# Windowed attention and a bilinear feed-forward layer: four more down projections by seven block products, with up weights and sums of w_out parked in HBM

## The chip, the cores and the metric

The kernel runs on one core of a Trainium2 chip. The metric is the device time of one execution in microseconds (us); the median of three runs of the kernel before is 953.4 us (953.39 to 955.16). Batches, blocks and products are counted from 0 in this text: the change concerns the down projections of batches 3, 4, 5 and 6 of 8, which are the fourth to the seventh.

## The reference

Eight batches with 8 heads, 576 tokens and 64 columns a head go through attention with a window of 128 tokens, and the result, 4608 tokens of 512 numbers, through a bilinear layer with 1536 hidden columns. All in float32.

```python
scores = scale * np.matmul(q, k.transpose(0, 1, 3, 2))
...
scores = np.where(mask, scores + bias[None], -1000000000.0)
...
return np.matmul(attn, v).astype(np.float32)
...
a = x @ w_a
b = x @ w_b
return (a * b @ w_out).astype(np.float32)
```

## The kernel before

**Numbers.** A float32 operand is split into two float16 numbers, a high and a low one, and each product of two such operands is three float16 matmuls. The token dimension of a batch is cut into two halves of `HT` = 288 tokens, so nearly every matmul of the layer is 128x128 weights by 288 columns.

**Stages of a batch.** Attention works on pairs of heads, four pairs a batch, and runs ahead of the layer. The *up* stage forms for each of 12 hidden blocks `f` both products with `w_a` and `w_b` and multiplies them (`up_fast`, line 1187). From batch 2 on it does this by seven block products of half size in place of eight (Strassen's scheme in Winograd's form): `wup[:, f]` holds seven operands for block f, the four given ones and three sums, each as high and low. `up` runs two lanes, the even and the odd blocks, interleaved. The *down* stage multiplies the hidden numbers with `w_out` (`wdn`). For batches 0 to 6 it does so directly (`down`, line 1257): 2 token halves x 4 output blocks x 12 hidden blocks x 3 = 288 matmuls. The last batch alone uses seven products there too (`down_fast`, line 1357): 7 x 2 x 6 x 3 = 252 matmuls. For this `Pairs.keep` (line 1324) forms, for each pair of hidden blocks, sums of their halves, called tops, and writes them over up weights that the last batch does not need again; `Pairs.weights` (line 1293) forms sums of w_out in buffers that attention no longer needs.

**After each product** ScalarE (ACT) or VectorE (DVE) takes the result out of PSUM. In the plain path `halve` (line 1145) then splits a hidden block with one ACT cast and one DVE subtraction of 2x288.

**What sets the order.** Every operation is recorded first (`Plan.record`), so all instructions carry one line of the program, 353; tiles tell them apart. `Plan.order` lists them by priorities (due times worked back from the end) and estimated costs, `arrange` (line 336) tries three settings of `early` with some repetitions each and keeps the best, and `emit` writes the instructions out in order of planned start. On the chip each engine runs its own list in that order and waits by semaphores. SyncE (SP) issues nearly all DMAs: an entry that waits holds back all entries behind it. `weave` and `att.along` set how attention, up and down are recorded beside each other.

**Names in rows.** `ch` and `ef` are PSUM banks of up and down, `at` those of attention; `rc`, `row` hold hidden numbers in float32, `stage` (also called h) the split hidden numbers of a batch, `xs` the split attention output, `phl` the split probabilities, `pT` their transposes by DMA, `qk`, `qkh`, `qkl`, `qst`, `v`, `vhl` the inputs of attention and their halves.

## Time and profile before

| | |
|---|---|
| runs | 955.16, 953.40, 953.39 us |
| the profiled execution | 953.69 us, of which its span is 951.9 us |
| TensorE (PE) busy | 938.8 us, 99% of the span, 9317 matmuls in the record |
| VectorE (DVE) busy | 721.6 us, 76% |
| ScalarE (ACT) busy | 652.4 us, 69% |
| GpSimd (POOL) busy | 277.7 us, 29% |
| mean granted TensorE clock | 0.996 of full speed |
| HBM read, written | 48.33 MB, 9.44 MB |

The profiled execution took 1.8 us more than its span and lies 0.3 us above the median. A busy time is the union of an engine's instructions; on DVE the recorded instructions overlap a little, so a group's mean is longer than the distance from one start to the next. Some matmul records can be missing.

### The profile page before, as it was taken

How to read it: one execution, taken by the hardware profiler on the slowest of the kernel's cores; microseconds unless marked ns; L12 is line 12 of the kernel's file. 1: busy time of each engine (PE TensorE's matmuls, PEld its weight loads, DVE VectorE, ACT ScalarE, POOL GpSimd, SP SyncE). 2: the span in 40 equal slices, each digit the busy share in tenths (PEclk: the TensorE clock that was granted, in tenths of full speed). 3: DMA queues.
4: the chain of work that ended last, by engine and by line, in shares of the span. 5: the costliest groups of instructions: out<-in, count | busy, mean ns of one | idle time of the engine just before them, and what ended most of it. 6: DMA issues, size and time to landing. Idle time of an engine off the chain costs nothing.

```text
span 951.9 us, 23890 instructions
## 1 busy us (share of the span) xinstructions
PE 938.8 (99%) x9317; PEld 742.3 (78%) x9317; DVE 721.6 (76%) x1955; ACT 652.4 (69%) x1737; POOL 277.7 (29%) x336
## 2 busy tenths in 40 slices
PE   7999999999999999999999999999999999999998
PEld 5777777777877877777777778778777777877776
DVE  4999998985888889956877577857767567488860
ACT  5979987676777777777757766777657766434431
POOL 1201021061677576301223122301222022362210
PEclk8999999999999999999999999999999999999999
DMA  9638563449536423554438344274336352200001
GB/s 355 189 126 275 157 133 106 155 86 217 131 78 183 96 46 80 111 155 101 89 56 213 71 98 95 71 180 94 72 71 134 117 93 32 49 33 7 2 7 45
DMA packets 150737, 104.90 MB, mean 110 GB/s; under 512 B 120160, under 2 KB 130016, under 8 KB 149728
## 3 DMA queue, kind: packets, MB, share of 16 engines
q1 hardware_dynamic: 141120, 93.83, 40.6%
q10 hardware_dynamic: 9504, 9.54, 3.1%
q8 instruction: 73, 1.20, 0.5%
q14 instruction: 40, 0.33, 0.1%
HBM read 48.33 MB, written 9.44 MB: 61 GB/s over the span
## 4 chain that ended last, share of the span: by engine, by line
PE 92%; DVE 3%; DMA 2%; issue 1%; ACT 1%; SPq 0%; DVEq 0%; ACTq 0%
PE ch L353 42%; PE ef L353 40%; PE at L353 11%; DMA qk<-in_kT 1%; DVE wup L353 1%; DMA stage<-in_kT 1%; DMA wdn<-in_w_b 1%; DVE small L353 0%; SPq L353 0%; DVE t L353 0%; DVE rc L353 0%; ACT qkh L353 0%; DVE qkl L353 0%; DVE xs L353 0%; ACT sq L353 0%
## 5 line engine op out<-in xcount | busy, mean ns | idle before, releaser
L353 PEld LDWEIGHTS <-wup 128*128 128x128 f16 x4176 | 403.1, 98 | 111.3 <-issue 4.5
L353 PE MATMUL ch<-xs,wup 128*128 128x288 f16 x2184 | 307.7, 286 | 0.7 <-ACT row L353 0.6
L353 PE MATMUL ef<-xs,wup 128*128 128x288 f16 x1992 | 284.7, 286 | 1.9 <-DVE wup L353 1.9
L353 PEld LDWEIGHTS <-wdn 128*128 128x128 f16 x2124 | 204.5, 98 | 54.6
L353 PE MATMUL ef<-stage,wdn 128*128 128x288 f16 x1080 | 138.1, 286 | 0.0
L353 ACT ACTIVATE t<-t,small 128x192 f32<-128x192 f32 (+2 forms) x276 | 118.3, 431 | 22.3 <-DVE small L353 21.7
L353 PE MATMUL ch<-stage,wdn 128*128 128x288 f16 x1008 | 130.1, 286 | 0.0
L353 DVE SCALAR_TENSOR_TENSOR phl<-t,small,phl 128x192 f16<-128x192 f32 (+2 forms) x252 | 109.0, 474 | 10.3 <-ACT phl L353 9.5
L353 POOL TENSOR_TENSOR rc<-rc,row 128x288 f32<-128x288 f32 x60 | 55.4, 923 | 209.9 <-DVE row L353 170.7
L353 ACT ACTIVATE phl<-t,small 128x192 f16<-128x192 f32 (+2 forms) x252 | 91.9, 427 | 6.6 <-DVE small L353 4.7
L353 DVE CUSTOM_DVE_ANT_0 t<-at,bias,small 128x192 f32<-128x192 f32 (+2 forms) x216 | 74.0, 390 | 21.1 <-PE at L353 20.3
L353 POOL TENSOR_TENSOR wup<-wup 128x128 f32<-128x128 f32 (+1 forms) x110 | 80.8, 760 | 25.6 <-DVE wup L353 17.0
L353 ACT ACTIVATE row<-ch,small 128x288 f32<-128x288 f32 x99 | 49.0, 495 | 54.9 <-PE ch L353 52.1
L353 ACT CAST stage<-rc 128x576 f16<-128x576 f32 (+1 forms) x81 | 52.3, 646 | 40.2 <-DVE rc L353 31.9
L353 DVE TENSOR_TENSOR stage<-rc,stage 128x576 f16<-128x576 f32 (+1 forms) x81 | 63.4, 782 | 7.5 <-ACT stage L353 6.3
L353 DVE SCALAR_TENSOR_TENSOR rc<-rc,small,ch 128x288 f32<-128x288 f32 x79 | 40.2, 509 | 32.7 <-PE ch L353 31.2
L353 POOL TENSOR_SCALAR bias<-rel_sb,small,sl_sb 128x192 f32<-128x192 f32 x24 | 19.3, 805 | 128.5 <-DVE small L353 128.5
L353 POOL TENSOR_TENSOR v<-v 128x576 f32<-128x576 f32 x24 | 34.9, 1453 | 60.6 <-ACT v L353 38.0
L353 ACT ACTIVATION_READ_ACCUMULATOR t<-t,small 128x1 f32 x276 | 52.5, 190 | 0.0
L353 DVE TENSOR_TENSOR xs<-v,xs 128x576 f16<-128x576 f32 x48 | 45.8, 973 | 8.3 <-ACT xs L353 8.3
L353 DVE SCALAR_TENSOR_TENSOR qkl<-qk,small,qkh 128x1152 f16<-128x1152 f32 x24 | 35.8, 1491 | 15.0 <-ACT qkh L353 13.1
L353 PEld LDWEIGHTS <-vhl 128*64 128x64 f16 x1176 | 39.9, 110 | 6.7 <-issue 6.4
(168 smaller groups left out, 1250.1 us busy)
## 6 DMA issues: line engine op xcount, KB each, us to landing
v<-in_vP SPq DMA_DIRECT2D x7, 1280.0 KB, 7.2
out<-row ACTq DMA_DIRECT2D x56, 144.0 KB, 2.7
qk<-in_qT SPq DMA_DIRECT2D x24, 288.0 KB, 4.0
qk<-in_kT SPq DMA_DIRECT2D x24, 288.0 KB, 4.7
wdn<-in_w_a SPq DMA_DIRECT2D x12, 512.0 KB, 6.3
wdn<-in_w_b SPq DMA_DIRECT2D x12, 512.0 KB, 8.0
wdn<-in_w_out SPq DMA_DIRECT2D x12, 512.0 KB, 6.0
qst<-qkh SPq DMA_DIRECT2D x24, 144.0 KB, 3.0
```

The lines of the kernel that those rows point to most:

```text
L353: getattr(eng, fn)(*args, **kw)
```

## The change

1. **Down by seven products from batch 3 on** (`Pairs.FIRST = 3`, `batch`). `up_fast` of these batches writes into `pair` tiles and calls `pairs.keep` in place of `halve`; `down_fast` gets all seven products in a new order, and its results leave through `stage` space, by SP's queue for all but the last batch.
2. **Up weights go to HBM and come back.** The tops of batches 3 to 7 are written over up blocks 1, 3, 5 and 7, the sums of w_out over blocks 6, 8 and 9. So these blocks (7 DMAs, 41 pieces of 131,072 bytes, 5.37 MB) are saved once while their sums are formed (`save`), and brought back after the down stages of batches 2 to 6 (`restore`, five times).
3. **Sums of w_out** are formed once, in batch 2's down stage, by DVE and ACT in up blocks already read, stored to HBM, and fetched again for each down stage (`fetch`, 3 DMAs, 2.36 MB, five times); one sixth of them stays in `wdn` from batch 3 on (`fetch_lasts`, 6 DMAs).
4. **The planner**: prices for DMAs that also count eight completion lanes, the bytes of each transfer and some stalls; a load from the parked copies may start up to 20 us ahead of its due time, others 100 us; and after the old trials 60 more with changed due times, of which the best stays.
5. **Rest**: `xs`, `rc` and the new `pair` tiles share one tile `rows`; the second half of the plain down outputs goes by SP from `stage` space; temporary places of the up sums are listed by hand (`turns`); the token scale's sums use an attention bank in paired batches.

```diff
 class Plan:
-            u.cost, u.lat = (4900.0, 4100.0) if kw.get("transpose") else (450.0, 4000.0)
+            u.ahead = 20000.0 if any(x.tensor.name in self.scratch for x in ins) else 100000.0
+            u.cost, u.lat = (4900.0, 4100.0) if kw.get("transpose") else (450.0, 3500.0 + u.line)
...
+        for n in range(60):
+            order, dues, self.zero, self.early = best[1]
+            dues = dict(dues)
+            for v, x in best[3]:
+                if rng.random() < 0.2:
+                    dues[v] -= x * rng.random() * 2
+            self.order(order, dues)
+            if self.end < best[0]:
+                best = keep()
...
     class Pairs:
+        FIRST = 3
+        TOPS, WEIGHTS = ((1, 0), (3, 0), (3, 1), (5, 0), (5, 1), (7, 0)), (6, 8, 9)
+        KEPT = ((1, 5), (3, 7), (5, 7), (7, 4), (6, 6), (8, 6), (9, 6))
+        UNIT = 512
...
+        def restore(self):
+            for f, k, to in self.blocks:
+                sp.dma_start(self.part(f, k), to)
+
+        def fetch(self, b):
+            for f, x in zip(self.WEIGHTS, self.loads):
+                sp.dma_start(self.part(f, 6), x)
...
         def weights(self):
...
+                for k, x in enumerate((a, c)):
+                    vec.tensor_tensor(out=x, in0=wdn[:, 2 * i + k, 0, :], in1=wdn[:, 2 * i + k, 1, :], op=ALU.add)
+                a11, a21, a12, a22 = (x[:, e:e + 256] for x in (a, c) for e in (0, 256))
+                vec.tensor_tensor(out=a22, in0=a21, in1=a22, op=ALU.add)
+                vec.tensor_tensor(out=a21, in0=a11, in1=a21, op=ALU.subtract)
+                vec.tensor_tensor(out=a11, in0=a22, in1=a11, op=ALU.subtract)
+                vec.tensor_tensor(out=a12, in0=a12, in1=a11, op=ALU.subtract)
                 yield
+                for z, w in ((a12, to[4]), (a22, to[2]), (a21, to[3]), (a11, to[1])):
+                    act.copy(w[:, 0, :], z)
+                    vec.tensor_tensor(out=w[:, 1, :], in0=z, in1=w[:, 0, :], op=ALU.subtract)
+                sp.dma_start(self.loads[i // 2][:, 3 * n * (i % 2):3 * n * (i % 2) + 3 * n], flat[:, n:4 * n])
+                sp.dma_start(self.lasts[:, i * n:i * n + n], flat[:, 4 * n:5 * n])
...
         def keep(self, f):
...
-            act.copy(tops[:, :, 0, :], x)
-            for n in (0, 2):
-                vec.tensor_tensor(out=tops[:, n:n + 2, 1, :], in0=x[:, n:n + 2, :], in1=tops[:, n:n + 2, 0, :], op=ALU.subtract)
+            first, rest = self.top(i, 0), self.top(i, slice(1, 4))
+            act.copy(first[:, 0, :], x[:, 0, :])
+            vec.tensor_tensor(out=first[:, 1, :], in0=x[:, 0, :], in1=first[:, 0, :], op=ALU.subtract)
+            act.copy(rest[:, :, 0, :], x[:, 1:4, :])
+            vec.tensor_tensor(out=rest[:, :, 1, :], in0=x[:, 1:4, :], in1=rest[:, :, 0, :], op=ALU.subtract)
...
     def down_fast(b, oi, p):
+        p.fetch(b)
...
+        yield from p.product(pss[0], 4, 0, True, True)
...
+        for j in range(2):
+            yield from p.product(chs[j], 5, j, False, True)
+            act.activation(xx[j][2], chs[j], AF.Copy, scale=oi)
...
+        yield from p.product(pss[1], 4, 1, True, True)
...
+        for j in range(2):
+            yield from p.product(pss[j], 2, j, False, True)
...
+        for j in range(2):
+            yield from p.product(chs[j], 3, j, False, True)
...
+        for j in range(2):
+            yield from p.product(chs[j], 6, j, False, True)
+            act.activation(xx[j][3], chs[j], AF.Copy, scale=oi)
+            out(j, 1, xx[j][3])
+        if b < B - 1:
+            p.restore()
...
     def batch(b):
+        paired = b >= pairs.FIRST
+        if b == pairs.FIRST:
+            pairs.fetch_lasts()
+        ups = up(states[b], None if paired else h, plain, fast)
...
+        if paired:
+            weave(att.along(down_fast(b, out_scale(states[b], states[b].g), pairs), 40, NPAIR * b + 6))
+        else:
+            weave(att.along(down(b, out_scales(states[b]), h, plain + fast), 48, NPAIR * b + 6), *((spread, *x) for x in quota[b][1]), *[(halved, 0, 40, 12)] * (b == pairs.FIRST - 1))
+        if b == pairs.FIRST - 1:
+            pairs.restore()
```

On PE the change issues 144 weight loads and 144 matmuls less than before, 36 of each in each of batches 3 to 6.

**SP, the end of batch 5's down stage and the start of batch 6's up stage, before.** `v` and `qk` are the next inputs of attention, `pT<-phl` is a transpose by DMA.

```order
L353 DMA qkh1_106<-qkh1_106 64x1152 [waits DMAHW6_49,DMAHW3_49]
L353 DMA qkl1_108<-qkl1_108 64x1152 [waits DMAHW7_49,DMAHW4_49]
L353 DMA_TRANSPOSE pT_90<-phl_87 128x32x128 [waits DMAHW1_49,DVE_49]
L353 DMA v_88<-in_vP 128x2560 [waits DVE_49]
L353 DMA qk_111<-in_qT 64x2x576 [waits DMAHW5_49,DVE_49]
L353 DMA qk_111<-in_kT 64x2x576 [waits DMAHW6_49,DMAHW2_49]
L353 DMA qst_112<-qkh0_105 64x1152 [waits DMAHW7_49,PE_49]
L353 DMA qst_112<-qkl0_107 64x1152 [waits DMAHW0_49]
```

**The same place now.** `keep1` and `keep3` are the parked copies of up blocks 1 and 3; the words in brackets are the engines and DMA lanes that an entry waits for.

```order
L397 DMA qkh1_116<-qkh1_116 64x1152 [waits DMAHW7_49,DMAHW1_49]
L397 DMA qkl1_118<-qkl1_118 64x1152 [waits DMAHW2_49,DMAHW0_49]
L397 DMA wup_80<-keep1_104 128x2560 [waits DMAHW3_49,PE_49]
L397 DMA v_90<-in_vP 128x2560 [waits DMAHW4_49,DVE_49]
L397 DMA_TRANSPOSE pT_92<-phl_89 128x32x128 [waits DMAHW5_49,DVE_49]
L397 DMA qk_121<-in_qT 64x2x576 [waits DMAHW6_49,DVE_49]
L397 DMA qk_121<-in_kT 64x2x576
L397 DMA wup_80<-keep3_105 128x3584 [waits PE_49]
L397 DMA qst_122<-qkh0_115 64x1152 [waits DMAHW1_49,PE_49]
L397 DMA qst_122<-qkl0_117 64x1152 [waits DMAHW2_49]
```

The restore of block 1 stands ahead of the load of v, that of block 3 behind two entries that wait for DVE; blocks 5 to 9 come later among attention's DMAs and eight outputs that ACT's queue carried before.

**DVE, the middle of a later up stage, before.** `stage<-rc` of 2x288 is the second half of `halve`, once for each block; `phl` belongs to attention.

```order
L353 TENSOR_TENSOR rc1_103<-ef0_74,rc1_103 128x288
L353 TENSOR_TENSOR rc0_102<-ch0_100,rc0_102 128x288
L353 SCALAR_TENSOR_TENSOR row0_113<-ef2_76,small_61,row0_113 128x288
L353 SCALAR_TENSOR_TENSOR rc0_102<-rc0_102,small_61,ch0_100 128x288
L353 SCALAR_TENSOR_TENSOR phl_87<-t0_91,small_61,phl_87 128x192
L353 TENSOR_TENSOR rc1_103<-ch1_101,rc1_103 128x288
L353 SCALAR_TENSOR_TENSOR phl_87<-t1_92,small_61,phl_87 128x192
L353 TENSOR_TENSOR stage_72<-rc0_102,stage_72 128x2x288
L353 SCALAR_TENSOR_TENSOR row1_114<-ef1_75,small_61,row1_114 128x288
```

**A like place now.** `rows` is the tile that `rc`, `xs` and `pair` share.

```order
L397 TENSOR_TENSOR rows_82<-rows_82 128x576
L397 SCALAR_TENSOR_TENSOR phl_89<-t3_96,small_61,phl_89 128x192 x2
L397 TENSOR_SCALAR small_61<-halves_77,small_61 128x2
L397 SCALAR_TENSOR_TENSOR phl_89<-t0_93,small_61,phl_89 128x128
L397 SCALAR_TENSOR_TENSOR phl_89<-t0_93,small_61,phl_89 128x64
L397 SCALAR_TENSOR_TENSOR vhl0_119<-v_90,small_61,vhl0_119 128x640
L397 TENSOR_TENSOR rows_82<-ef1_75,rows_82 128x288
L397 TENSOR_TENSOR stage_72<-rows_82,stage_72 128x2x288
L397 TENSOR_TENSOR rows_82<-ch0_102,rows_82 128x288
L397 TENSOR_TENSOR rows_82<-rows_82 128x288
L397 SCALAR_TENSOR_TENSOR row0_123<-ef0_74,small_61,row0_123 128x288
L397 TENSOR_TENSOR stage_72<-rows_82,stage_72 128x288
```

What was one subtraction of 2x288 a block is, over a pair of blocks, 128x576 and 2x288 once each, 128x288 four times and 3x288 once.

**DVE, a little after batch 3's token scale, before.** The rows are attention's alone.

```order
L353 SCALAR_TENSOR_TENSOR phl_87<-t0_91,small_61,phl_87 128x128
L353 SCALAR_TENSOR_TENSOR phl_87<-t0_91,small_61,phl_87 128x64
L353 SCALAR_TENSOR_TENSOR phl_87<-t1_92,small_61,phl_87 128x192 x2
L353 SCALAR_TENSOR_TENSOR phl_87<-t2_93,small_61,phl_87 128x192 x2
L353 RECIPROCAL small_61<-small_61 128x2
L353 CAST small_61<-small_61 128x4
L353 SCALAR_TENSOR_TENSOR phl_87<-t3_94,small_61,phl_87 128x192 x2
L353 TENSOR_SCALAR small_61<-halves_77,small_61 128x2
L353 ISA t0_91,small_61<-at2_98,bias_95,small_61 128x64
```

**A like place now.** `wup<-wdn` and `wup<-wup` are sums of w_out and their low halves, formed in up blocks.

```order
L397 TENSOR_TENSOR wup_80<-wdn_81 128x512
L397 TENSOR_TENSOR wup_80<-wup_80 128x256 x3
L397 CAST small_61<-small_61 128x4
L397 TENSOR_TENSOR wup_80<-wup_80 128x256
L397 RECIPROCAL small_61<-small_61 128x2
L397 TENSOR_TENSOR wup_80<-wup_80 128x256
L397 SCALAR_TENSOR_TENSOR phl_89<-t0_93,small_61,phl_89 128x192
L397 SCALAR_TENSOR_TENSOR phl_89<-t0_93,small_61,phl_89 128x128
```

Of the 60 DVE instructions that form these sums 9 stand ahead of batch 3's token scale and 51 between it and batch 4's, 9 of 512 columns and 42 of 256 columns.

## Rows read from the trace of the kernel before

**Rows 1.** The page: busy us of each engine (share of the span) xinstructions.

```profile
PE 938.8 (99%) x9317; PEld 742.3 (78%) x9317; DVE 721.6 (76%) x1955; ACT 652.4 (69%) x1737; POOL 277.7 (29%) x336
```

**Rows 2.** The chain that ended last, by engine.

```profile
PE 92%; DVE 3%; DMA 2%; issue 1%; ACT 1%; SPq 0%; DVEq 0%; ACTq 0%
```

**Rows 3.** The waits of TensorE: total us, times, longest us.

```profile
PE at L353 <- DMA stage<-in_kT: 3.1, 1, 3.1
PE at L353 <- DVE small L353: 2.9, 3, 2.2
PE ef L353 <- DVE wup L353: 1.9, 2, 1.3
```

**Rows 4.** Windows from one token-scale reduction to the next: length, busy per engine.

```profile
293.00:396.50 103.50, 102.86 (x1033) 81.43 (x1031) 91.81 (x230) 78.61 (x210) 66.61 (x87) 1.00 0.43 101
396.50:506.00 109.50, 109.43 (x1108) 86.85 (x1106) 80.60 (x239) 79.45 (x217) 24.83 (x25) 1.00 0.49 107
506.00:616.30 110.30, 110.30 (x1117) 87.67 (x1116) 77.75 (x236) 78.65 (x215) 23.47 (x24) 1.00 0.47 105
...
726.60:836.50 109.90, 109.90 (x1088) 87.49 (x1087) 70.55 (x194) 67.56 (x182) 25.68 (x24) 1.00 0.38 80
```

**Rows 5.** Windows: one up phase, one down phase, two early stretches.

```profile
519.80:588.00 68.20, 68.20 (x698) 54.50 (x697) 46.87 (x140) 50.83 (x137) 12.75 (x14) 1.00 0.44 94
588.00:630.20 42.20, 42.20 (x422) 33.27 (x420) 30.99 (x97) 27.92 (x78) 10.79 (x10) 1.00 0.53 124
0.00:25.00 25.00, 18.68 (x196) 14.29 (x198) 11.16 (x46) 15.07 (x49) 4.94 (x23) 0.86 0.94 358
75.00:100.00 25.00, 25.00 (x224) 18.55 (x221) 24.59 (x78) 24.87 (x70) 2.84 (x8) 1.00 0.75 229
```

**Rows 6.** The chain in order of time, the end: start us, us, what.

```profile
930.91 2.21 PE ch L353 x18
...
948.59 0.50 ACT rc L353
```

**Rows 7.** Vector instructions of the last batch by form: busy us, mean ns.

```profile
L353 DVE TENSOR_TENSOR wup<-v,wup 128x576 f16<-128x576 f32 x8 | 7.6, 976 | 0.1
...
L353 DVE TENSOR_TENSOR v<-v 128x288 f32<-128x288 f32 x8 | 3.6, 454 | 0.2
...
L353 DVE TENSOR_TENSOR v<-v 128x576 f32<-128x576 f32 x4 | 3.0, 757 | 0.1
L353 DVE TENSOR_TENSOR stage<-v,stage 128x576 f16<-128x576 f32 x4 | 3.0, 757 | 0.0
...
L353 DVE TENSOR_TENSOR stage<-v,stage 128x288 f16<-128x288 f32 x4 | 1.8, 446 | 0.0
```

**Rows 8.** The same for one middle batch.

```profile
L353 DVE TENSOR_TENSOR stage<-rc,stage 128x576 f16<-128x576 f32 x12 | 9.3, 779 | 1.5 <-ACT stage L353 1.2
L353 DVE TENSOR_TENSOR xs<-v,xs 128x576 f16<-128x576 f32 x7 | 6.6, 959 | 0.0
...
L353 DVE SCALAR_TENSOR_TENSOR rc<-rc,small,ch 128x288 f32<-128x288 f32 x12 | 6.1, 511 | 7.5 <-PE ch L353 7.2 <-PE at L353 0.2
```

**Rows 9.** The timeline of VectorE where it runs without a pause.

```profile
553.26 0.46 DVE L353 TENSOR_TENSOR rc<-ef,rc 128x288 f32<-128x288 f32 x1
553.64 0.45 DVE L353 SCALAR_TENSOR_TENSOR phl<-t,small,phl 128x192 f16<-128x192 f32 x1
```

**Rows 10.** DMA issues: KB each, median us to landing.

```profile
qst<-qkl SPq DMA_DIRECT2D x24, 144.0 KB, 3.9
...
v<-in_vP SPq DMA_DIRECT2D x2, 640.0 KB, 7.8
...
pT<-phl SPq DMA_TRANSPOSE x28, 7.5
```

**Rows 11.** The waits at the head of the SP queue.

```profile
SPq L353 <- DVE phl L353: 171.2, 23, 17.9
```

**Rows 12.** Products of GpSimd in one middle batch.

```profile
L353 POOL TENSOR_TENSOR rc<-rc,row 128x288 f32<-128x288 f32 x12 | 10.6, 885 | 46.3 <-DVE row L353 38.1 <-DVE small L353 6.6 <-ACT qkl L353 1.5
```

More of the change, by code (lines that the diff above doesn't have):

```diff
@@ L4 @@
 from itertools import chain, cycle
+from random import Random
 from types import SimpleNamespace
@@ L263, in order @@
             if not left[u]:
-                ready[u] = max(0.0, u.due - zero - self.ahead) if u.load else 0.0
+                ready[u] = max(0.0, u.due - zero - u.ahead) if u.load else 0.0
                 heappush(wait[u.eng], (ready[u], u.n, u))
@@ L292, in order @@
                     u, t = soon[3], max(t, soon[1])
+            u.late = free[e], t - ready[u]
             t = max(t, ready[u])
@@ L336, in arrange, with keep @@
     def arrange(self):
-        best = None
+        best, rng = None, Random(1)
+        def keep():
+            return self.end, self.made, {u: u.start for u in self.units}, self.late()
         for self.early in (3000.0, 4000.0, 5000.0):
@@ L343, in arrange, with late @@
                 if best is None or self.end < best[0]:
-                    best = self.end, {u: u.start for u in self.units}
+                    best = keep()
[7 more added lines that the diff above has]
+            if self.end < best[0]:
+                best = keep()
         self.end = best[0]
         for u in self.units:
-            u.start = best[1][u]
+            u.start = best[2][u]
+    def late(self):
+        out = []
+        for u in self.units:
+            gap = u.start - u.late[0]
+            if u.eng != "tensor" or u.loose or gap < 100.0:
+                continue
+            v = u.cause
+            for _ in range(8):
+                if v is None or v.eng == "tensor":
+                    break
+                if v.late[1] > 50.0:
+                    out.append((v, min(gap, v.late[1]) + 200.0))
+                v = v.cause
+        return out
     def emit(self):
@@ new lines, in __init__, with unit @@
+            self.h, self.tiles = h, {}
+            self.blocks = [(f, k, self.scratch(k * self.UNIT, f"keep{f}")) for f, k in self.KEPT]
+            self.loads = [self.scratch(6 * self.UNIT, f"sums{f}") for f in self.WEIGHTS]
+            self.lasts = self.scratch(NF // 2 * self.UNIT, "lasts")
+        def unit(self, i, k):
+            if k == 3:
+                return wdn[:, 2 * i, :, 256:512]
+            return view(wup[:, self.WEIGHTS[i // 2], 3 * (i % 2) + (1, 2, 0)[k]].rearrange("p n k c -> p (n k c)"), [P, 2, 256], F16)
@@ new lines, in scratch, with part, save @@
+        def scratch(self, n, name):
+            t = store.tile([P, n], F16, name=name)
+            plan.scratch.add(t.tensor.name)
+            return t
+        def part(self, f, k):
+            return wup[:, f, 0:k].rearrange("p m n k c -> p (m n k c)")
+        def save(self, f):
+            for n, k, to in self.blocks:
+                if n == f:
+                    sp.dma_start(to, self.part(f, k))
+        def restore(self):
+            for f, k, to in self.blocks:
+                sp.dma_start(self.part(f, k), to)
@@ L1321, in hidden, with tile, top @@
+        def tile(self):
+            return work.tile([P, 4, HT], F32, tag="pair", name="pair")
+        def top(self, i, n):
+            if n == 0:
+                return self.h[:, 2 * i, 1]
+            f, n0 = self.TOPS[i]
+            x = self.part(f, 7)[:, 6 * HT * n0:6 * HT * n0 + 6 * HT]
+            return x.rearrange("p (n w s) -> p n w s", n=3, w=2)[:, n - 1 if isinstance(n, int) else slice(n.start - 1, n.stop - 1)]
         def hidden(self, f):
-            return self.fp32[f // 2 % 3][:, 2 * (f % 2):2 * (f % 2) + 2, :]
+            if f % 2 == 0:
+                self.tiles[f // 2] = self.tile()
+            return self.tiles[f // 2][:, 2 * (f % 2):2 * (f % 2) + 2, :]
```

176 lines of the change are left out of this document (82 added, 94 removed).

## The prediction

> **What bounds the kernel now.** The order of reading was: the page's busy shares, the chain that ended last, TensorE's waits, windows from one batch to the next, and the rows of single instructions. TensorE is busy 938.8 of 951.9 us and nothing else comes near [rows 1]; 92% of the chain is its own work [rows 2]. Its named waits are a few single ones in the first 200 us, 3.1 us for the first inputs the largest [rows 3]. From one token scale to the next a batch takes 109.5 to 110.3 us, and TensorE is busy for all of that but 0.07 us [rows 4]. So in the middle a matmul taken out is time taken out, as long as the other engines and the DMAs keep their lead. The nearest of them is VectorE: 77.75 of 110.3 us in a batch, 91.81 of 103.5 in the stretch that also forms sums of weights [rows 4], 46.87 of 68.2 in an up phase and 30.99 of 42.2 in a down phase [rows 5].
>
> **Part 1, the matmuls.** 18 matmuls of 128x288 take 2.21 us on the chain [rows 6], 122.6 ns each. 4 batches x 36 are 144 matmuls: 144 x 122.6 = 17.6 us. All of it lies on the path, since TensorE is without gaps in these four batches [rows 4]. The weight loads that go with them lie beside matmuls and give nothing more (PEld is busy 87.67 of 110.3 us [rows 4]). The last batch has seven products already; its tail is one ACT instruction of 0.50 us and a store [rows 6], and stays: product 6 of the second half is still last. Term: -17.6.
>
> **Part 2, VectorE's work for the tops, batches 3 to 6.** Per pair of blocks `keep` runs two subtractions of 2x288 or 128x576 (757 ns each), four of 288 (two at 454, two at 446) and one of 3x288, which has no row: from 454 and 757 the slope is 1.05 ns a column, so 1.06 us. That is 1.51 + 1.80 + 1.06 = 4.37 us [rows 7]. What goes is two halves of 779 ns, 1.56 us [rows 8]. Net 2.81 us x 6 pairs = 16.9 us a batch. Down gains six instructions of 511 ns [rows 8], 3.1 us. So VectorE has 77.75 + 16.9 + 3.1 = 97.8 us in a batch that takes 110.3 - 4.4 = 105.9, 92%; in the up phase 46.87 + 16.9 = 63.8 of 68.2, 94%. This is the upper end: without pauses the starts of two instructions lie 0.38 us apart where the first lasts 0.46 [rows 9], so a packed VectorE needs about 0.08 us less for each of some 270 instructions, 76 us in all. At both ends it fits. Where it was 89% busy (91.81 of 103.5), TensorE lost 0.64 us [rows 4]; in an earlier stretch it was busy 24.59 of 25 us and TensorE lost nothing [rows 5]. I take 0.7 us for each of batches 4 to 6, nearest the first of these rows: +2.1. Bounds 0 and, were each up phase stretched by a fifth of its new work, +10.
>
> **Part 3, the sums of w_out.** 51 of the 60 new instructions stand between batch 3's token scale and batch 4's, 9 of 512 columns and 42 of 256. By 757 ns for 576 and 454 for 288 [rows 7] they last about 0.68 and 0.42 us, 23.8 us together. That stretch has the tops of batch 3 too: 80.60 [rows 4] + 16.9 + 3.1 + 23.8 = 124.4 us at the upper end. Packed, at 0.08 us off each of 326 instructions, it is 98. The time that TensorE needs there is 109.4 - 4.4 = 105.0. So VectorE lies between 7 us under and 19 us over. The row at 98% busy [rows 5] shows that the packed end can nearly be reached, and part of the sums can slip, since the up blocks in which they lie are wanted one after the other through 60 us of batch 3's up. I take +4, nearer the packed end; bounds 0 and +19. This is the term I trust least.
>
> **Part 4, the DMAs.** A batch gains 5.37 + 2.36 = 7.73 MB in ten DMAs. The first 25 us moved 358 GB/s at a busy share of 0.94 [rows 5]; at that rate it is 21.6 us of all queues, 0.20 of a batch, on top of 0.47 [rows 4]. Room is there. Time: block 1 is last read in the first three matmuls of the last part of product 2; 15 more of it, 72 of products 3 and 6 and 24 of block 0 of the next up come before block 1 is wanted: 111 x 122.6 ns = 13.6 us, plus what attention puts between. A load of 640 KB, just that size, landed in 7.8 us in the crowded start [rows 10]. It stands behind copies that wait for each other's landing (3.9 us [rows 10]), so some 12 us in all. Later blocks are wanted 10 us apart, 84 matmuls. Term 0, because what hides the restore is products 3 and 6 and the head of up; with that cover gone, each restore costs about 8 us. Saves and stores of sums write to HBM, and nothing waits for them within 60 us. Bounds 0 and +40 for five restores.
>
> **Part 5, start and planner.** The start is issued in another order: the first q load is third in place of first, two issues later, and the first half of v stands ahead of it, so the first scores may come up to 2 us later, or the wait of 2.9 us on the scale of v [rows 3] may shrink by as much. ScalarE, at 78.65 of 110.3 us [rows 4], casts 2016 columns a pair of blocks in place of 1152; even at VectorE's 1.05 ns a column that is 5.4 us a batch, 84 of 105.9. TensorE's gaps outside the first 25 us and the last 3.3 are 3.5 us in all (951.9 - 938.8 less 6.3 and 3.3); longer trials of orders may close some. Term -1, bounds -3.5 and +2.
>
> **Sum.** 953.7 (the profiled execution) - 17.6 + 2.1 + 4 + 0 - 1 = 941.2; the profiled execution lies 0.3 above the median, so 941.
>
> **The rule weighed.** The sums and the tops read both operands from SBUF. In the rows such subtractions take 976 and 959 ns where GpSimd works beside them, and 757 where it doesn't [rows 7, 8]. The Trainium skill (SBUF — State Buffer, "Who interferes with whom") says that a Vector instruction with two SBUF inputs and a GpSimd instruction that reads SBUF exclude each other for a whole instruction. The rows agree in direction only: 0.2 us and not a whole instruction of GpSimd, which lasts 885 ns [rows 12]. By the rows the 30 new subtractions of a batch would cost VectorE at most 30 x 0.2 = 6 us more; by the rule the twelve products of GpSimd in a batch could hold it for up to 12 x 0.885 = 10.6 us.
>
> **Rivals.**
> *VectorE becomes the bound.* If the 30 new subtractions of a batch also take 0.2 us longer, VectorE's up phase is 63.8 + 6 = 69.8 of 68.2 us: some 1.5 us a batch in batches 3 to 6, and the stretch with the sums costs 8. Time 953.7 - 17.6 + 6 + 8 - 1 = 949. For it: 92 to 94%, where 89% cost 0.64. Against it: 98% without loss. Chance 0.16.
> *The restores come late, and the kernel gets slower.* The place is blocks 1, 3 and 5 at the head of each up. The head of SP's queue waited 23 times for the probabilities of attention, 171.2 us, 7.4 on average and 17.9 at most [rows 11]; a restore behind such an entry, 7.4 + 7.8 = 15.2 us after its block is free, is late by 1.6, and behind the longest by 12. At 7 us for each of five the time is 941 + 35 = 976; it decides from (17.6 - 5 + 1.9) / 5, about 3 us each. Against it: block 1 stands ahead of v and the transpose in the new order, and block 3 is wanted 10 us later. The Trainium skill (DMA: Bandwidth & Descriptors, "Issuing engines are not separate DMA queues") adds that all queues share the same 16 engines, so that restores and transposes also lengthen each other; a transpose takes 7.5 us already [rows 10]. Chance 0.09.
> *It does not do what it says: attention sets the pace.* Matmuls of the layer fill TensorE while scores, softmax and transposes of a pair of heads go round; with 36 fewer in a down phase the ring shows and the gain is waited away. Time 952 to 954. For it: transposes wait on VectorE. Against it: no wait of TensorE on attention in rows 3 outside the start. Chance 0.05.
> *All of the gain.* VectorE packs, the new orders close old gaps: 953.7 - 17.6 - 1 = 935. Chance 0.10.
> The forecast, 937 to 946, has 0.60.
>
> **How the numbers follow.** About 0.2%, 1.9 us, is what a measurement of this kernel can tell from no change. Faster by more: forecast 0.60, all of the gain 0.10, VectorE 0.15, a little of the others 0.02: 0.87. Within: 0.04 from attention and 0.01 from late restores that just eat the gain, 0.05. Slower: 0.08, late restores. The range takes in the forecast, most of the full gain and most of VectorE's case: 935 to 950.
>
> **What would show it.** In the changed profile: 144 fewer matmuls; from token scale to token scale about 106 us in batches 4 to 6 with TensorE busy all but 1 us, VectorE 92%; 107 to 111 us from batch 3's to batch 4's, with TensorE's waits on `ch` or `ef` releases by VectorE there and nowhere else. Wrong would be: waits of weight loads of `wup` on DMAs at the head of up; gaps before scores or `pT`; TensorE's gaps of more than 2 us in each of batches 4 to 6; a first 60 us longer by more than 2 us.

## The result, and the profile after

The changed kernel took 937.4 us (937.23 to 938.45) beside 953.8 for the kernel before: a ratio of 0.9828, 95% interval 0.9811 to 0.9845. A second measurement, made beside the experiments that leave work out, gave 937.65 against 950.86: 0.9861, 0.9844 to 0.9877. The changed kernel's time is nearly the same in both; it is the kernel before that differs, by 2.9 us, and its median stayed between 950.7 and 951.2 beside all experiments, on three chips. So the gain is 16.4 us in the first measurement and 13.2 in the second. The terms of the prediction add up to 12.5.

The page of the changed kernel, busy times of each engine, which answers to [rows 1]:

```profile
PE 920.3 (98%) x9173; PEld 727.1 (78%) x9173; DVE 785.3 (84%) x2123; ACT 668.0 (71%) x1803; POOL 266.0 (28%) x324
```

The 144 matmuls are gone to the last one, TensorE is busy 18.5 us less, and VectorE is at 84% in place of 76. TensorE's waits (total us, times, longest), which answer to [rows 3]:

```profile
PE at L397 <- DMA stage<-in_qT: 2.2, 1, 2.2
...
PE at L397 <- DMA qkh<-qkh: 1.0, 1, 1.0
PE at L397 <- DMA pT<-phl: 1.0, 1, 1.0
```

The list has no large wait, but DMAs of attention's inner tiles (`qkh`, `pT`), absent before, now stand in it. Where the time went is read from windows cut at a mark that both kernels have: TensorE's first matmul of the up stage of batches 2 to 7. Before (window, its length, busy us of PE, PEld, DVE, ACT and POOL with instruction counts, clock, DMA share, GB/s):

```profile
0.00:306.60 306.60, 297.53 (x3067) 232.55 (x3068) 260.39 (x723) 238.79 (x651) 97.71 (x150) 0.99 0.60 170
306.60:417.90 111.30, 110.66 (x1115) 87.58 (x1114) 94.44 (x250) 83.79 (x227) 57.94 (x74) 1.00 0.46 104
417.90:528.40 110.50, 110.43 (x1116) 87.64 (x1114) 78.79 (x236) 80.46 (x220) 23.51 (x23) 1.00 0.47 105
528.40:638.70 110.30, 110.30 (x1117) 87.68 (x1115) 77.72 (x234) 78.50 (x214) 23.44 (x23) 1.00 0.47 105
638.70:748.90 110.20, 110.20 (x1116) 87.61 (x1114) 77.65 (x234) 78.63 (x214) 23.45 (x23) 1.00 0.47 105
748.90:855.80 106.90, 106.90 (x1042) 85.38 (x1041) 73.33 (x171) 57.92 (x145) 36.67 (x30) 1.00 0.24 48
```

The same stretches after:

```profile
0.00:303.10 303.10, 295.41 (x3067) 230.90 (x3068) 258.64 (x720) 237.03 (x648) 103.37 (x158) 1.00 0.64 178
303.10:415.80 112.70, 110.85 (x1115) 87.65 (x1114) 100.11 (x280) 87.66 (x244) 52.06 (x66) 1.00 0.56 140
415.80:523.10 107.30, 106.25 (x1081) 84.26 (x1079) 103.65 (x283) 80.80 (x222) 24.80 (x22) 1.00 0.71 190
523.10:630.20 107.10, 106.20 (x1080) 84.31 (x1078) 96.38 (x282) 83.50 (x229) 25.85 (x24) 1.00 0.75 186
630.20:737.40 107.20, 106.08 (x1080) 84.31 (x1079) 95.60 (x270) 82.15 (x225) 25.37 (x23) 1.00 0.69 175
737.40:840.40 103.00, 102.61 (x1005) 81.81 (x1003) 80.66 (x194) 64.26 (x168) 25.02 (x20) 1.00 0.58 160
```

Down the two lists the lengths change by -3.5 (start and batches 0, 1), +1.4 (batch 2), -3.2, -3.2, -3.0, -3.9 (batches 3 to 6), and +0.2 in the last batch: -15.2, the difference of the spans. In batches 3 to 6 TensorE is busy 4.18 + 4.10 + 4.12 + 4.29 = 16.7 us less, and stands idle 1.05 + 0.90 + 1.12 + 0.39 = 3.5 us where it had stood idle 0.07. Batch 2 adds 1.2 us of idle time (1.85 against 0.64).

The -3.5 at the start is 2.1 us less busy time (297.53 to 295.41) and 1.4 less idle time, and the clock has a large part in the first. Before, TensorE waited 3.10 us for k, and then ran at half clock; timeline of TensorE before (start, us, what, wait ahead of it), and a window:

```profile
9.92 1.54 PE L353 MATMUL at<-stage 64*64 64x64 f32 x12 [3.10 <-DMA stage<-in_kT]
...
12.44 1.54 PE L353 MATMUL at<-stage 64*64 64x192 f32 x8
```

```profile
12.00:16.00 4.00, 4.00 (x27) 2.52 (x25) 1.25 (x10) 3.24 (x13) 0.42 (x1) 0.50 1.02 416
```

After, the wait is 2.19 us, and the same eight matmuls take 0.87:

```profile
6.98 2.35 PE L397 MATMUL at<-stage 64*64 64x64 f32 x32 [2.19 <-DMA stage<-in_qT]
...
10.22 0.87 PE L397 MATMUL at<-stage 64*64 64x192 f32 x8
```

The 6.1 us of work from 9.9 to 16 us, at a granted clock of 0.50 (the level of 1.2 GHz), would by estimate have taken half as long, so 3.0 us were lost; of the whole stretch's busy time 2.1 us went. The kernel before was 2.9 us slower in the first measurement than beside the experiments, where no trace of it was taken. Its mean clock was 0.996 in the profiled execution of the first measurement and 0.998 or more in 44 of the 52 runs beside the experiments. The eight runs at 0.996 among those have a median of 952.1 us, those at 0.998 one of 950.9. So the clock accounts for some 1.3 of the 2.9 us by estimate, and the rest stays open.

### The profile page after: what moved, and what is told of

It is laid out like the page before. It is cut to its first block, busy times and chain, and to the rows that moved or that the text cites. A ratio compares the mean times of both kernels' runs of the same rounds, so it can differ in the third digit from the quotient of the medians.

```text
span 936.7 us, 23891 instructions
## 1 busy us (share of the span) xinstructions
PE 920.3 (98%) x9173; PEld 727.1 (78%) x9173; DVE 785.3 (84%) x2123; ACT 668.0 (71%) x1803; POOL 266.0 (28%) x324
## 4 chain that ended last, share of the span: by engine, by line
PE 78%; DMA 10%; DVE 6%; ACT 3%; issue 1%; SPq 1%; POOL 0%; DVEq 0%; ACTq 0%
PE ch L397 36%; PE ef L397 34%; PE at L397 9%; DMA pT<-phl 3%; DVE wup L397 1%; DVE rows L397 1%; DMA stage<-in_kT 1%; DMA qk<-in_kT 1%; DMA v<-in_vP 1%; DMA qkl<-qkl 1%; DVE t L397 1%; DVE phl L397 1%; DVE small L397 1%; DMA wdn<-in_w_a 1%; DMA wdn<-in_w_b 1%
## 5 line engine op out<-in xcount | busy, mean ns | idle before, releaser
L397 PEld LDWEIGHTS <-wup 128*128 128x128 f16 x4716 | 455.0, 98 | 127.3 <-issue 7.1
L397 PE MATMUL ch<-rows,wup 128*128 128x288 f16 x2184 | 304.2, 286 | 2.4 <-ACT row L397 1.1
L397 PE MATMUL ef<-rows,wup 128*128 128x288 f16 x1992 | 279.4, 286 | 0.9 <-DVE wup L397 0.9
L397 PEld LDWEIGHTS <-wdn 128*128 128x128 f16 x1584 | 152.9, 98 | 40.3
L397 POOL TENSOR_TENSOR rows<-rows,row 128x288 f32<-128x288 f32 x72 | 71.9, 998 | 289.7 <-DVE row L397 242.7
L397 ACT CAST stage<-rows 128x288 f16<-128x288 f32 (+1 forms) x123 | 65.8, 539 | 46.7 <-DVE rows L397 37.6
L397 PE MATMUL ef<-stage,wdn 128*128 128x288 f16 x648 | 84.2, 286 | 0.0
L397 DVE TENSOR_TENSOR stage<-rows,stage 128x576 f16<-128x576 f32 (+1 forms) x123 | 79.8, 654 | 4.0 <-ACT stage L397 3.2
L397 DVE TENSOR_TENSOR rows<-rows 128x288 f32<-128x288 f32 (+2 forms) x96 | 58.3, 614 | 0.7
L397 DVE TENSOR_TENSOR rows<-v,rows 128x576 f16<-128x576 f32 x48 | 48.0, 1015 | 5.1 <-ACT rows L397 5.1
```

The costliest lines, as they stand in the source:

```text
L397: getattr(eng, fn)(*args, **kw)
```

## The experiments

### The planner and the start

**The kernel before with the new planner.**

```diff
-class Unit, class Plan            # of before
+class Unit, class Plan            # of the changed kernel: DMA prices, ahead, 60 trials
```

> The kernel before with the planner of the change alone (its DMA prices, its load-ahead times and its 60 more trials); the program that is planned is that of before. Theory S (the start): some 3.5 of the 15.2 us by which the changed kernel's profiled span is shorter lie ahead of batch 2's up stage and come from the planner, which issues the first inputs in another order; then this kernel takes 953.8 - 3.5 = 950 us, TensorE waits less than 2.5 us in one piece for its first inputs and the granted clock is 1.00 throughout the first 25 us. Rival M (the start is better because of the other edits, the places of tiles and of sums): 953 to 955 us, with the wait of 3.1 us and the clock at half from 10 to 16 us as before. Rival T (the trials close the old gaps all over): 949 or less, with TensorE's idle time outside the first 25 us below 2 us.

949.56 us, ratio 0.9990 (0.9981 to 0.9999). TensorE's longest wait for its first inputs was 1.6 us, and the clock was 1.00 up to 20 us, 0.66 from 20 to 25. So the shorter wait and the 950 us came as theory S said, a clock of 1.00 throughout did not: it fell later, behind the wait of 1.6 us at 19 us. The gain on this chip was 1.5 us in medians and 1.0 in the ratio, not 3.5. The mean clock, 0.998 in the median run of either kernel, shows no gain of clock here.

**The changed kernel with the old planner.**

```diff
-class Unit, class Plan            # of the changed kernel
+class Unit, class Plan            # of before; parked copies still tracked
```

> The changed kernel with the planner of before (old DMA prices, every load up to 100 us ahead, no further trials). Theory S: the start is that of before, the rest that of the changed kernel: 937.4 + 3.5 = 941 us, with the clock at half for some 6 us ahead of 20 us. Rival M: 937 to 938 us with the clock at 1.00 from the start. Rival D (the new prices are needed to keep restores out of attention's way): 944 us or more, with TensorE waiting for DMAs in batches 4 to 6 for over 2 us in each.

988.49 us, ratio 1.0401 (1.0382 to 1.0420): rival D, and far beyond its figure. TensorE's two largest entries (total, times, longest):

```profile
PE at L354 <- DMA qkh<-qkh: 20.5, 2, 11.4
PE at L354 <- DMA wup<-keep: 10.2, 1, 10.2
```

That is one wait of 9 to 11 us in each of batches 4 to 6 (11.4, 10.2, 9.1), and the clock fell behind them (mean 0.977 of the execution). The prediction's second rival, restores that come late, is real, though two of the three waits are on a copy of attention and one on a restore: what keeps it away is the order, and the order is the new planner's.

**Without the 60 trials.**

```diff
-        for n in range(60):
+        for n in range(0):
```

> The changed kernel with the new prices but none of the 60 further trials. If the prices make the better start: within 1 us of 937.4, clock 1.00 at the start. If the trials make it: 940 to 942 us, with the clock at half at the start. If the trials close gaps later: TensorE idle after 300 us is 7 us or more in place of 5 to 6, and the time 938 to 940 us.

940.14 us, ratio 0.9886 (0.9873 to 0.9900), 2.5 us more than the changed kernel in medians from two chips; the intervals just overlap. The clock at the start was 1.00 in the trace, so the prices make the start. That the trials close gaps later is not shown: TensorE's idle time from 300 us to the last batch was 5.9 us, 5.3 with the trials, and not the 7 expected. In the trace, the fastest of the four runs, batch 3 took 108.8 us (107.3 with the trials) and batch 6 103.7 (103.0), but batch 4, with all its restores and tops, 105.8 (107.1) and no wait.

**The kernel before, the gap at the start filled.**

```diff
+            if first and u.eng == "tensor":
+                first = False
+                for _ in range(26):
+                    eng.matmul(*u.calls[0][1], **u.calls[0][2])
```

> The kernel before with 26 more of the matmuls on constants with which TensorE begins (60 in place of 34, 0.11 us each, 2.9 us), everything else in the same order. Theory C (the clock): in before the clock fell to half after TensorE had stood idle for 3.1 us, and the matmuls from 10 to 16 us lost 3.0 us by it; with the gap filled the clock stays at 1.00 and the time is 953.8 - 3.0 = 951 us, or up to 952 if the first scores, 2.9 us later, hold VectorE up. Rival O (what counts is when the inputs come, and the clock falls anyway): 953 to 955 us. Rival L (all of the start moves by what is added): 956 to 957 us.

950.76 us, ratio 0.9995 (0.9986 to 1.0004): no gain on this chip, and no test of theory C: its 951 us came, but the kernel before took 951.01 here without the filling. The clock was 1.00 from 8 to 16 us, but the next wait for k, 2.10 us, ended at 19.2 us, and the clock fell there:

```profile
12.00:16.00 4.00, 4.00 (x61) 3.19 (x60) 3.68 (x11) 4.00 (x18) 0.06 (x1) 1.00 1.02 407
...
20.00:22.00 2.00, 2.00 (x15) 1.12 (x13) 1.53 (x12) 2.00 (x7) 0.00 (x0) 0.50 1.05 390
```

### What costs TensorE 1 us a batch

These kernels keep every instruction of the changed one in its place and leave some out.

**The changed kernel again.** 

> The changed kernel as it is, beside the kernel before on the same chip: what the three kernels below are compared with. If the time of before differs from chip to change of chip by what its clock does in the first 25 us (951.0 beside the first four experiments, 953.8 beside the first measurement), the ratio here lies between 0.983 and 0.986; if all that the changed kernel gained holds on every chip, it is 0.983 again.

937.65 against 950.86 us, 0.9861 (0.9844 to 0.9877), as above: at the upper edge of what was expected if the kernel before differs, and not 0.983 again.

**Without restores after batches 3 to 6.**

```diff
         def restore(self):
+            plan.drop = plan.batch >= self.FIRST
             for f, k, to in self.blocks:
                 sp.dma_start(self.part(f, k), to)
+            plan.drop = False
```

> The changed kernel, every instruction in the same order, without the 28 DMAs that bring the up blocks back after the down stages of batches 3 to 6 (the up stages of batches 4 to 7 then read the tops and sums that were left there). Theory V (what TensorE loses in batches 3 to 6, some 1 us a batch, is lost to VectorE): within 0.7 us of the changed kernel. Rival X (it is lost to restores that hold up attention's DMAs or the next up stage): 2 to 3 us less, and TensorE's idle time below 0.4 us in each of batches 4 to 6 in place of 0.9, 1.1 and 0.4.

934.84 us, ratio 0.9831 (0.9816 to 0.9845): 2.8 us less, rival X.

**Without the tops of batches 3 to 6.**

```diff
+            plan.drop = plan.batch < B - 1
             vec.tensor_tensor(out=x[:, 0:2, :], in0=x[:, 1:4:2, :], in1=x[:, 0:2, :], op=ALU.subtract)
+            plan.drop = False
...
+            plan.drop = plan.batch < B - 1
             vec.tensor_tensor(out=x[:, 3, :], in0=x[:, 3, :], in1=x[:, 0, :], op=ALU.subtract)
...
             vec.tensor_tensor(out=rest[:, :, 1, :], in0=x[:, 1:4, :], in1=rest[:, :, 0, :], op=ALU.subtract)
+            plan.drop = False
```

> The changed kernel, every instruction in the same order, without the instructions of VectorE and ScalarE that sum and split the tops in batches 3 to 6 (the down stages then read what stood in those places). Theory V: TensorE's idle time falls to 0.3 us or less in each of batches 3 to 6, 2.5 to 3.5 us less in all. Rival X: within 0.7 us of the changed kernel, the waits on DMAs stay.

934.69 us, ratio 0.9833 (0.9818 to 0.9847): 3.0 us less, the time of theory V, with batch 3 idle for more (0.56 us) than it allowed.

**Without the sums of w_out.**

```diff
+                plan.drop = True
                 for k, x in enumerate((a, c)):
                     vec.tensor_tensor(out=x, in0=wdn[:, 2 * i + k, 0, :], in1=wdn[:, 2 * i + k, 1, :], op=ALU.add)
...
+                plan.drop = False
                 sp.dma_start(self.loads[i // 2][:, 3 * n * (i % 2):3 * n * (i % 2) + 3 * n], flat[:, n:4 * n])
```

> The changed kernel, every instruction in the same order, without the instructions of VectorE and ScalarE that form the sums of w_out in batch 2's down stage and batch 3's up stage (what lies in the up blocks is stored in their place). By the prediction these sums cost 4 us: 4 us less. By the trace of the changed kernel, in which TensorE stands idle 1.85 us in batch 2 and 1.05 in batch 3 where it did 0.64 and 0.07 before, at most 2 us less. Rival P (the sums lie in VectorE's pauses, and the idle time is that of another order of the plan): within 0.5 us of the changed kernel.

934.75 us, ratio 0.9833 (0.9819 to 0.9848): 2.9 us less, more than the trace had seemed to allow.

Each of the three takes away about the same 3 us (every one of their runs lies below the changed kernel's fastest, 937.04), and TensorE's idle time in batches 3 to 6 of the changed kernel on this chip was 2.6 us in all. So the prices don't add. TensorE's idle time in us, from windows cut at the mark used above:

| batch | 3 | 4 | 5 | 6 |
|---|---|---|---|---|
| changed kernel | 1.03 | 0.97 | 0.44 | 0.19 |
| without restores | 1.12 | 0 | 0 | 0 |
| without tops | 0.56 | 0.05 | 0 | 0.21 |
| without sums | 0.27 | 0 | 0 | 0 |

Batch 3 and batches 4 to 6 differ. In batch 3 nearly all is one wait for a transpose of attention; TensorE in the changed kernel, then without tops:

```profile
467.30 1.54 PE L397 MATMUL at<-pT,vhl 128*64 128x128 f16 x42 [0.98 <-DMA pT<-phl]
```

```profile
466.81 1.54 PE L401 MATMUL at<-pT,vhl 128*64 128x128 f16 x42 [0.56 <-DVE small L401]
```

It stays without restores (0.95) and is gone without sums, so there the loss comes from VectorE's load. In batches 4 to 6 the restores are needed for it. Batch 4 as an example, up and down stage, first the changed kernel, then without restores (batches 4, 5 and 6), then without sums:

```profile
522.30:629.70 107.40, 106.43 (x1080) 84.43 (x1078) 97.14 (x283) 83.77 (x233) 24.98 (x24) 1.00 0.76 189
```

```profile
523.10:628.90 105.80, 105.80 (x1080) 84.11 (x1078) 96.34 (x283) 83.61 (x233) 25.86 (x24) 1.00 0.58 141
628.90:734.70 105.80, 105.80 (x1080) 84.12 (x1078) 95.44 (x270) 83.30 (x227) 26.73 (x23) 1.00 0.55 130
734.70:837.20 102.50, 102.50 (x1006) 81.86 (x1005) 80.69 (x194) 63.39 (x166) 25.02 (x20) 1.00 0.39 97
```

```profile
521.60:627.50 105.90, 105.90 (x1081) 84.18 (x1080) 96.22 (x282) 83.18 (x230) 25.83 (x24) 1.00 0.74 189
```

Without restores VectorE has as much to do as ever in batch 4, 96.34 us, and TensorE loses nothing; without sums the batch has all its restores and all its tops, and loses 0.0 us. The waits of batch 4 show why. In the changed kernel ScalarE comes to the square of the next q and k at 565.5, the load of k is not there, and the product row behind it in ScalarE's order (at 567.41) is late for TensorE; timeline of ScalarE, then of TensorE:

```profile
566.25 1.17 ACT L397 ACTIVATE qkl<-qk 128x1152 bf16<-128x1152 f32 x1 [0.79 <-DMA qk<-in_kT]
```

```profile
567.95 0.90 PE L397 MATMUL ch<-rows,wup 128*128 128x288 f16 x6 [0.67 <-ACT row L397]
```

Without restores the same square starts with no wait:

```profile
565.75 1.17 ACT L401 ACTIVATE qkl<-qk 128x1152 bf16<-128x1152 f32 x1
```

The load had been issued late and landed late. In SP's queue it stands behind a restore, two copies and the load of q; rows of SP (issue, us in the queue) in the changed kernel, then without sums, and the changed kernel's row of the load among the DMA issues (KB, us to landing):

```profile
557.38 1.46 SPq L397 DMA_DIRECT2D qst<-qkl  x1
...
559.62 0.64 SPq L397 DMA_DIRECT2D qk<-in_kT  x1
```

```profile
556.44 0.52 SPq L401 DMA_DIRECT2D qst<-qkl  x1
...
557.74 0.64 SPq L401 DMA_DIRECT2D qk<-in_kT  x1
```

```profile
qk<-in_kT SPq DMA_DIRECT2D x1, 288.0 KB, 6.5
```

The landing, 6.5 us after the issue, was 4.6 without restores and 6.3 without sums. Without sums the restore lengthens it as well, but the copy ahead of it took 0.52 us of the queue in place of 1.46, and the load is there in time. What held that copy, some engine's or lane's signal, the rows don't tell. Over the batches from 4 on copies of q and k landed later too. Median us from issue to landing from 520 to 840 us, changed kernel, then without restores:

```profile
qst<-qkh SPq DMA_DIRECT2D x10, 144.0 KB, 5.1
...
pT<-phl SPq DMA_TRANSPOSE x12, 8.4
```

```profile
qst<-qkh SPq DMA_DIRECT2D x10, 144.0 KB, 3.4
...
pT<-phl SPq DMA_TRANSPOSE x12, 8.3
```

So batch 4 is a race lost by 0.8 us: the restore makes the load late, and each of three reliefs that move the queue and ScalarE against each other wins it. That the sums, formed a batch earlier, act by a lag of VectorE carried into batch 4 is inferred, not shown. The waits of batches 5 and 6, 0.6 us together, were not followed in this way.

### Moving the cost

**Restores issued by ScalarE.**

```diff
-            eng = getattr(self.nc, u.eng)
+            eng = self.nc.scalar if u.aside else getattr(self.nc, u.eng)
```

> The changed kernel, every instruction in the same place, but the 28 DMAs that bring up blocks back after batches 3 to 6 are issued by ScalarE and not by SyncE. Theory F (attention's copies qst, qkh and qkl land late, 4.5 to 4.8 us against 2.8 to 4.2 without these DMAs, because they stand behind them in one queue): they land in 3 to 4 us again and the time is 1.5 to 2.5 us less than that of the changed kernel (937.7 beside before at 950.9). Rival E (what they share is the DMA engines, whatever queue issues them): landing stays at 4.5 to 5 us, the time within 0.7 us. Rival A (ScalarE stands still at each of these DMAs until its block has been read): TensorE waits for ScalarE in batches 4 to 7, 2 us or more slower.

949.06 us, ratio 0.9989 (0.9962 to 1.0015), 945 to 957: nearly the whole gain is lost, and why the runs spread so far is open. The copies qkh and qkl landed in 3.1 and 3.6 us, as theory F said, but the two of qst both in 4.9 (5.1 and 4.8 with SP alone), the loads of qk in 5.9 and 6.4 (4.0 and 4.6) and pT in 9.3. TensorE's largest wait, and a wait of ScalarE that was 2.0 us in all with SP alone:

```profile
PE at L399 <- DMA pT<-phl: 5.7, 4, 3.3
```

```profile
ACT phl L399 <- DMA pT<-phl: 16.8, 7, 3.4
```

The lateness moved from some of the copies to the loads and transposes. The time is that of rival A, and TensorE did wait for ScalarE (1.6 us at 534 us, 1.5 at 757), but ScalarE's own waits there are for transposes, not for blocks to be read. The Trainium skill (DMA: Bandwidth & Descriptors, "Issuing engines are not separate DMA queues") says that transfers issued by different engines run on the same 16 engines and interleave; the loads of qk, which SP issued as before and which landed 1.9 us later, agree.

**Each restore twice.**

```diff
-            for fn, args, kw in u.calls:
+            for fn, args, kw in u.calls * (1 + u.twice):
```

> The changed kernel, every instruction in the same order, with each of the 28 DMAs that bring up blocks back after batches 3 to 6 issued twice in a row. Theory F: attention's copies land later still, 6 us or more, and TensorE's idle time in batches 4 to 6 doubles from some 2.5 us to 5: 940 to 941 us. Rival W (the up blocks themselves come too late): waits for wup<-keep show at the head of each up stage and the time is 945 us or more. Rival H (all of it is hidden; the waits of batches 4 to 6 are VectorE's): within 0.7 us of the changed kernel.

1012.83 us, ratio 1.0661 (1.0634 to 1.0688): the time of rival W, 75 us more than the changed kernel where it named 7 or more. But the up blocks are the smaller part of TensorE's waits, and attention's copies, once issued, landed in 4.2 to 5.3 us, not the 6 of theory F. TensorE's waits, and the wait at the head of SP's queue:

```profile
PE at L399 <- DMA qkh<-qkh: 17.6, 5, 6.0
...
PE at L399 <- DMA pT<-phl: 12.5, 3, 6.4
PE ch L399 <- DMA wup<-keep: 5.4, 1, 5.4
```

```profile
SPq L399 <- DMA wup<-keep: 145.3, 31, 7.7
```

The second copy waits in SP's queue until the first has landed, 4.7 us on average, and everything of attention waits behind it. So it tests a held queue more than doubled bytes. TensorE's mean clock fell to 0.975 as well: in batches 4 to 6 its idle time grew by 54 us and its busy time by 18.5.

**Sums of w_out added on GpSimd.**

```diff
-                    vec.tensor_tensor(out=x, in0=wdn[:, 2 * i + k, 0, :], in1=wdn[:, 2 * i + k, 1, :], op=ALU.add)
-                vec.tensor_tensor(out=a22, in0=a21, in1=a22, op=ALU.add)
+                    pool.tensor_tensor(out=x, in0=wdn[:, 2 * i + k, 0, :], in1=wdn[:, 2 * i + k, 1, :], op=ALU.add)
+                pool.tensor_tensor(out=a22, in0=a21, in1=a22, op=ALU.add)
...
```

> The changed kernel with the 36 additions and subtractions of the sums of w_out (12 of 512 and 24 of 256 columns) on GpSimd in place of VectorE, the 24 splits of the results still on VectorE; the order is planned anew. VectorE has some 18 us less to do in batch 2's down and batch 3's up stage. Theory V (VectorE's load there starts the waits): the idle time of batches 3 and 4 falls as without the sums, 1.5 to 2.5 us less than the changed kernel. Rival G (GpSimd's longer instructions and VectorE's hold each other up): the mean of VectorE's subtractions of 2x288 and 576 columns in batch 3 rises by 0.2 us or more and the time is 1 to 5 us more.

942.87 us, ratio 0.9919 (0.9902 to 0.9936): 5 us worse, theory V's gain did not come. Rival G named the size, but not the place: in batch 3 VectorE's subtractions of 2x288 took 750 ns, 748 in the changed kernel. What shows is a new order with two waits for VectorE, 0.90 us at 434 and 2.39 at 437 us, and a fallen clock around them. VectorE was busy with attention's rows from 431.4 to 436.5 us, ahead of the row that the second wait is for, and GpSimd stood idle from 427.7 to 438.7, so these waits are not two engines holding each other up. TensorE, timeline and window:

```profile
437.07 1.60 PE L397 MATMUL ch<-rows,wup 128*128 128x288 f16 x6 [2.39 <-DVE rows L397]
```

```profile
430.00:445.00 15.00, 11.70 (x129) 8.78 (x129) 11.84 (x43) 12.29 (x40) 1.97 (x1) 0.77 0.78 256
```

**Eight restores later in SP's queue.**

```diff
+        for r in [u for u in order if u.later]:
+            ...                                   # past q's and k's DMAs that follow it
+            order.insert(j + 1, r)
+            del order[i]
```

> The changed kernel with eight of the 28 restores of batches 4 to 7 (blocks 8 and 9 in three batches, block 3 in two) put two to four places later in SP's queue, behind the copies and loads of attention's q and k that stood right after them; all else in the same order. Theory F (these copies land late because they stand behind a restore, and so ScalarE's square of q and k and the product behind it start late): the wait of 0.7 us of TensorE near 568 us goes, that on qkh near 672 too, and the time is 1 to 2 us less than the changed kernel's 0.986 of before. Rival E (the waits come from the bytes that share the engines, not from the place in the queue): within 0.7 us. Rival L (the restores, now up to 6 us later, are late themselves, or hold up the transposes behind them): TensorE waits for wup or pT in batches 4 to 6, 2 us or more slower.

941.27 us (938.21 to 943.12), ratio 0.9887 (0.9869 to 0.9905), 3.6 us more in medians, with an interval that just overlaps the changed kernel's: rival L by its waits. The wait on row near 568 us is gone; in its place the restore itself is late, then the transpose behind it, then qkh a batch on:

```profile
567.37 0.91 PE L413 MATMUL ef<-rows,wup 128*128 128x288 f16 x6 [0.96 <-DMA wup<-keep]
576.74 2.06 PE L413 MATMUL at<-pT,vhl 128*64 128x128 f16 x41 [2.06 <-DMA pT<-phl]
677.15 0.22 PE L413 MATMUL at<-qkh,qst 128*64 128x64 f16 x2 [1.53 <-DMA qkh<-qkh]
```

No version tried here that does the whole computation beats the changed kernel.

## Why the prediction was right, and where it was not

**Matmuls, -17.6.** Right. Without restores TensorE has no wait in batches 4 to 6, and these take 105.8, 105.8 and 102.5 us where they took 110.3, 110.2 and 106.9 before: 4.4 us for 36 matmuls, 123 ns each, the 122.6 of the forecast. The 16.7 us by which busy time fell in the changed kernel, 116 ns each, is less because busy time grows beside waits (batch 4: 106.43 us with them, 105.80 without). What is taken out of a gapless TensorE is taken out of the time.

**VectorE's tops, +2.1, and the sums, +4.** The load was right: 97.8 us forecast for a batch, 96.4 and 95.6 measured in batches 4 and 5; 98 to 124 for the stretch of the sums, 103.65 measured, 97% of 107.3. The price was right in sum only, and by luck: batches 3 to 6 became 13.3 us shorter, not 17.6, and batch 2 1.4 longer, which makes 5.7 us for the 6.1 forecast. The split and the path were wrong. The row that priced the tops, 0.64 us lost where VectorE was 89% busy, was no price of VectorE: nearly all of it is one wait for ScalarE, and with the new planner alone that batch lost 0.05 us. TensorE before:

```profile
386.73 0.90 PE L353 MATMUL ch<-xs,wup 128*128 128x288 f16 x6 [0.56 <-ACT row L353]
```

Of the 4 us expected where the sums stand, batch 3 lost 1.0 in idle time and batch 2 1.2. The waits were forecast on `ch` and `ef`, released by VectorE; batch 3's is on a transpose of attention, and gaps before `pT` and scores were among the signs of being wrong. Batch 2's idle time, which lies at 314 to 328 us, ahead of the sums, was the same without sums, without tops and without restores (1.85 us in each). What causes it stays open.

**DMAs, 0.** This step failed. It asked whether an up block would be wanted before its restore had landed, and no such wait is in the trace, as said. It did not price what the restore does to the entries behind it in the queue: copies of q and k that land 0.6 to 1.7 us later in the median, in batch 4 a load that lands 1.9 us later, and through these 2.8 us in all. The terms were added as if each engine lost time by itself; in batch 4, the largest part, the runs show one late load that needs the restore, the tops and the sums together, and a wait that goes with any of them.

**Start and planner, -1.** By the new planner alone it was 1.0 us (0.1 to 1.8), as forecast. The 3 us more of the first measurement come from the kernel before, by estimate 1.3 of them by its clock. The sum held that time for part of every execution. The low clock was in the row of 0.86 for the first 25 us [rows 5] and went unused.

**The rivals.** Late restores did not happen, but the mechanism is real, and its price of 7 us for each return of the blocks was low for a held queue: with each restore issued twice, four returns cost 75 us, 19 each, and in the old planner's order the kernel took 51 us more than in the new one. What it named as late, the up blocks, was the smaller part; most of the waits were for attention's DMAs. Attention setting the pace came in small: of the 2.6 us of idle time in batches 3 to 6, 1.7 stand ahead of attention's matmuls and 0.9 ahead of others that waited for ScalarE. VectorE as the bound, at 97% in batch 3, cost there the 1.0 us that is gone without sums, not 8.

**The rule weighed.** The prediction found that the rows agree with the rule in direction only, by 0.2 us. That was a reading of means. Single instructions of VectorE (two subtractions with both inputs in SBUF) and of GpSimd in batch 4 show the exclusion itself:

```profile
566.10 0.45 DVE L397 TENSOR_TENSOR rows<-rows 128x288 f32<-128x288 f32 x1
566.46 1.05 DVE L397 TENSOR_TENSOR stage<-rows,stage 128x288 f16<-128x288 f32 x1
```

```profile
566.26 0.94 POOL L397 TENSOR_TENSOR rows<-rows,row 128x288 f32<-128x288 f32 x1 [6.37 <-DVE row L397]
```

The one that started ahead of GpSimd's took 0.45 us, as without it; the one that started during it ended 0.3 us after it. In batches 4 and 5, 26 such subtractions of 288 columns that met no GpSimd instruction took at most 458 ns, 22 that met one up to 1528; those with one input in PSUM took at most 458 either way. The price stayed below the bound all the same, since only 11 of these 48 took over 0.5 us: with 25.85 us of GpSimd's work in batch 4, those of 288 columns rose on the mean to 670 and 590 from 446 and 454 in [rows 7], 12 x 0.22 + 12 x 0.14 = 4.3 us, nearer the 6 that the rows gave than the 10.6 worked out from the Trainium skill (SBUF — State Buffer, "Who interferes with whom"), and the batch's load stayed below the forecast with it.

## What to carry to other kernels

Where the bounding engine has no gaps, work taken from it is worth its time, and the question is which queue the replacement lengthens: follow what stands behind each new DMA, not only who waits for its data. Prices of parts that meet in one race can't be added; leaving each out in turn, with the order of all else held, shows whether they share a wait. The cover of a transfer has an edge: with 28 more queue entries, held 4.7 us on average until the one ahead had landed, the kernel took 75 us more.

## What the runs showed of the hardware

With restores of 512 to 896 KB in the queue, copies of 144 KB in the same queue landed up to 1.7 us later in the median, but transposes by DMA as without them (8.4 and 8.3 us). A wait of TensorE can cost twice: after 3.10 us at the start, after 2.10 us in the kernel with the gap filled, and about the waits of 0.90 and 2.39 us in the middle of the kernel with sums on GpSimd, the granted clock fell to 0.50 or, over a 15 us window, 0.77. With the new planner alone it fell after 1.6 us at 19 us (0.66 from 20 to 25). After 2.19 us of waiting at the start of the changed kernel it did not fall. A VectorE subtraction of 288 columns with both inputs in SBUF took 0.45 us, and 1.05 where it started during an instruction of GpSimd.
